# The second pair's keys turned on VectorE with unscaled tables, merged table products, zeros from ScalarE, one low weight part on VectorE, and a new order of all operations

## The chip, the cores and the metric

The kernel runs on one core of a Trainium2 chip. The metric is device microseconds of one execution; a median of three is given. TensorE is called PE in the rows, VectorE DVE, ScalarE ACT, GpSimd POOL, and the engine whose queue starts most transfers SP.

## What is computed

An attention over 8 batches and 8 heads (576 positions, 64 numbers a head) with rotary positions feeds a gated MLP. In short:

```python
q_rot, k_rot = (rotate(q), rotate(k))          # x1*cos - x2*sin, x1*sin + x2*cos
scores = scale * np.matmul(q_rot, k_rot.transpose(0, 1, 3, 2))
attn = softmax(scores)
x = np.matmul(attn, v)                          # heads side by side: (8, 576, 512)
h = np.maximum(x @ w_in, 0.0)                   # 512 -> 1024
u, v = (h[..., :512], h[..., 512:])
v_n = (v - mean(v)) / sqrt(var(v) + 1e-6)
v_s = einsum('ts,bsd->btd', w_spatial, v_n) + b_spatial
out = (u * v_s) @ w_out
```

## The kernel before

Heads are worked in 32 pairs, four pairs to a batch. A pair's q and k come transposed, 128 rows (two heads of 64) by 2 x 576 columns: the numbers and their swapped halves. The rotation is one product of all 1152 columns with the cosine and sine tables `tabs`, and one sum of the two halves of 576. Pairs 0 to 3 (`prepare_whole`, WHOLE = 4) feed plain float32 products; later pairs (`prepare`) are split into a high and a low part and stacked for three-term products. Scores of one tile (128 queries by 576 keys) fill two banks of PSUM, which has eight (`sc` buffers of two banks, `pm` buffers of one). On each tile VectorE takes the maximum (line 843) and ScalarE the exponential (line 846); only then are the banks free. For pairs 0 to 3 TensorE then transposes the weights (lines 684 and 687), VectorE or ScalarE copies them out (lines 693 and 695) and TensorE multiplies them with the values (line 730); later pairs use VectorE's transposes (line 848) and line 761. When the four pairs of a batch are done, `mlp` runs: lines 918 (v half), 941 (u half), 959 (spatial) and 974 (output), interleaved with the next batch's attention. The scaling by 1/8 is split between q and k: the tables are multiplied by the square root of 1/8 (line 643) once pair 0 has been turned, and pair 0's keys take the whole 0.125 instead.

The weights come as 64-bit numbers and are decoded by VectorE and ScalarE (`decode`), with a high part rounded by ScalarE and the rest subtracted on POOL (lines 468 and 469, through the helper at 423). `open_stacks` (line 397) fills two half tiles with zeros on POOL before pair 4. At the very start four matmuls on zeros (`wake`, line 1034) keep TensorE busy until the first scores.

Every operation is recorded in a list and then issued in the order of the text `ORDER`, one number per operation. A letter picks the engine where there is a choice (a ScalarE, v VectorE, g POOL); `HOME` gives the slot of each new buffer, PSUM banks included. Each engine, and each queue, takes its own operations in that order, so a waiting one holds back all that follow on its engine.

Of the kernel before, what the change touches and what calls it, by code (L numbers as in the profile page):

```python
# [40 lines left out]
DEC_O = [120.69, 119.26, 149.95, 144.74]  # L41
GATE_U = [2, 2, 3, 3]
# [58 lines left out]
0 2 4 6 5 1 3 7 12 66 10 8 9 139 11 143 16 14 17 140 309 13 15 71 72 77 75 73 74 76 82 80 81 145 78 79 18 87 60 61 141 85 86 83 84 88 89 90 219 144  # L101
146v 92 91 93 94 131 19 313 97 101 98v 215 102a 142g 37 20 21 148 151 149 113 114a 95 96a 311 99 100a 104 105a 150 132 22 110 111a 133 23 24 103 152
424 25 106 107a 108 109a 503 38 153 63 221 156 39 154 127 128a 122 157 155 28 40 41 42 43 123a 112 124 158 394 220 222 134 62 125a 216 147 29 217 159
117 118a 161 119 120a 135 30 31 115 160 162 32 33 34 121 126 129 315 223 163 314 116 166 64 130 171 164 175 172a 167 310 312 165 218 176v 317 35 168
169 170 173 174v 177 178a 224 227 207 180 316 182 181a 186 421 46 228 184 300 225 226 185v 187a 183a 208 179 209 47 48 136 189 190v 229 230 137 44 232
49 50 51 188 422 428 231 203 204a 233 138 191 192 195 196a 385 193 194v 429 234 200 432 436 198 199a 52 235 236 45 201v 434 435 197 202 26 237 239 205
242 238 206 240 247 248v 244 245 243 256 257v 210 241 249 253 55 27 246 211 212 213 283 437 251 433 258 254v 259a 250v 252a 291 292 293 284 318 260
262 255 261a 423 430 431 319 320 321 322 265 214 53 54 323 263a 264 266a 294 295 269 296 297 438 439 271 324 325 326 327 274 298 412 275a 267 285 426
272v 328 268 301 302 270v 276 277a 329 330 273 279 280a 278 748 754 755 331 341 332 749 756 757 286 342a 303 304 305 444 36 345 346a 442 306 307 308
333 334 335 336 337 338 339 340 377 443 281 343 344v 440 446 447 441 287 378 347 348a 413 448 379 450 494 451 359 360a 356 357a 282 288 458 459 354  # L110
355v 820 826 445 449 349 452 380 453 352 381 350 460 414 415 462 463 454 351a 353a 363 365 764 765 416 455 417 364a 464 358 373 466 366a 418 767 368
289 290 374a 467 461 768 456 369a 370 403 386 367 361 419 371a 372 375 468 362 457 420 387 376 465 382 821 470 758 469 759 478 471 427 472 383 479 384
# [210 lines left out]
def tile_attention_gated_mlp(  # L323
# [102 lines left out]
    win, wout = {}, {}  # L426

    def decode(key, where, at, src, after=()):

        n = f"w{'io'[where is wout]}" + "".join(map(str, at))  # L430
        tiles = {}
        sg = Buf("m", [P, HF], I32, f"sg{n}")
# [694 lines left out]
```

## Time and profile before

| what | value |
| --- | --- |
| median of 3 runs | 813.5 us (813.34 to 813.94) |
| the profiled execution | 812.71 us |
| its span, first to last instruction | 810.9 us |
| TensorE matmul busy | 797.8 us (98%) |
| TensorE weight loads | 720.8 us (89%) |
| POOL / VectorE / ScalarE busy | 610.0 / 579.5 / 538.9 us |
| granted TensorE clock | 1.00 of 2.4 GHz in every slice |

The span leaves 1.8 us of the execution outside. A matmul's end is modelled, so a busy TensorE can still hide short pauses; the time at which the next matmul begins is exact. A line can be that of a helper: 423 is every low part, 420 every rounding, 388 every fill.

### The profile page before, as it was taken

Reading aid. Unit: us, or ns where it says so; the run is one execution under the profiler, and the core shown is the slowest. Engines: PE = TensorE matmul, PEld = TensorE weight load, DVE = VectorE, ACT = ScalarE, POOL = GpSimd, SP = SyncE. Lnnn points to the kernel's source line nnn. Section 1 sums busy time; section 2 is a strip of 40 time slices with the busy share of each in tenths; the row PEclk is TensorE's granted clock in tenths of the full one; section 3 lists DMA queues with packets and bytes.
Section 4 is the critical chain, followed back from the end, with each engine's and each line's share of the span. In section 5 each row is a group of like instructions: output and inputs, shape, how many; then the busy total and the mean of one; then the engine's idle time right before and its main releaser. Section 6 shows DMA issues by size and latency. Waiting matters only on the chain.

```text
span 810.9 us, 30065 instructions
## 1 busy us (share of the span) xinstructions
PE 797.8 (98%) x12568; PEld 720.8 (89%) x12568; DVE 579.5 (71%) x1230; ACT 538.9 (66%) x1355; POOL 610.0 (75%) x507
## 2 busy tenths in 40 slices
PE   7999999999999999999999999999999999999998
PEld 3666699988999989999999988999799998999898
DVE  6989998858876587677866769876696758774310
ACT  5889797656865577556875668766576657754442
POOL 7979899877798777887878868888687869643222
PEclk9999999999999999999999999999999999999999
DMA  9855575566676575567656667566656766453101
GB/s 346 276 167 172 141 195 124 143 186 171 161 183 172 152 196 152 169 167 190 174 148 170 163 181 197 148 173 159 168 149 152 186 180 179 101 123 84 44 2 59
DMA packets 53818, 129.85 MB, mean 160 GB/s; under 512 B 7858, under 2 KB 9906, under 8 KB 53683
## 3 DMA queue, kind: packets, MB, share of 16 engines
q1 hardware_dynamic: 53138, 127.35, 57.0%
q8 instruction: 98, 1.61, 0.8%
q10 hardware_dynamic: 544, 0.59, 0.2%
q14 instruction: 38, 0.30, 0.1%
HBM read 93.55 MB, written 9.58 MB: 127 GB/s over the span
## 4 chain that ended last, share of the span: by engine, by line
PE 86%; DMA 6%; POOL 4%; ACT 2%; issue 1%; DVE 1%; SPq 1%; ACTq 0%; POOLq 0%; DVEq 0%
PE psum L801 16%; PE psum L761 15%; PE psum L959 15%; PE psum L941 13%; PE psum L974 12%; PE psum L918 10%; DMA st<-in_qk_dram 2%; POOL st L545 2%; PE psum L821 2%; PE psum L684 1%; PE psum L730 1%; DMA ws<-in_w_spT_dram 1%; POOL st L549 1%; DMA vr<-in_v_dram 1%; DMA stk<-lk 1%
## 5 line engine op out<-in xcount | busy, mean ns | idle before, releaser
L846 ACT ACTIVATE et<-psum,nmx 128x576 f32<-128x576 f32 x288 | 212.7, 740 | 103.0 <-DVE nmx L843 100.4
L843 DVE TENSOR_REDUCE nmx<-psum 128x1 f32<-128x576 f32 x288 | 212.2, 747 | 85.9 <-PE psum L801 68.4
L848 DVE STREAM_TRANSPOSE et<-et 128x576 f32<-128x576 f32 x252 | 186.4, 760 | 31.4 <-ACT et L846 30.3
L545 POOL TENSOR_TENSOR st<-st,tabs 128x1152 f32<-128x1152 f32 x56 | 149.6, 2671 | 23.4 <-DMA st<-in_qk_dram 21.7
L761 PE MATMUL psum<-et,vr 32*64 32x144 f32 x8064 | 142.0, 285 | 0.5 <-DMA vr<-in_v_dram 0.5
L761 PEld LDWEIGHTS psum<-et,vr 32*64 32x64 f32 x8064 | 126.6, 130 | 12.0 <-issue 8.9
L959 PE MATMUL psum<-wsp,vn 128*128 128x288 f32 x768 | 126.6, 296 | 1.1 <-issue 1.1
L941 PE MATMUL psum<-x,wi 128*128 128x288 f32 x768 | 124.5, 296 | 0.4 <-issue 0.4
L918 PE MATMUL psum<-wi,x 128*128 128x512 f32 x448 | 120.6, 395 | 0.0
L974 PE MATMUL psum<-g,wo 128*128 128x288 f32 x768 | 120.2, 296 | 0.4 <-POOL g L423 0.4
L941 PEld LDWEIGHTS psum<-x,wi 128*128 128x128 f32 x768 | 110.8, 188 | 5.7 <-issue 2.3
L959 PEld LDWEIGHTS psum<-wsp,vn 128*128 128x128 f32 x768 | 109.8, 188 | 2.9 <-issue 2.2
L974 PEld LDWEIGHTS psum<-g,wo 128*128 128x128 f32 x768 | 108.4, 188 | 3.9 <-issue 2.0
L801 PE MATMUL psum<-stk 128*128 128x288 f32 x448 | 99.0, 302 | 2.0 <-ACT et L846 1.5
L801 PE MATMUL psum<-stk,stk 128*128 128x288 f32 x448 | 95.8, 295 | 0.6 <-issue 0.6
L918 PEld LDWEIGHTS psum<-wi,x 128*128 128x128 f32 x448 | 78.3, 188 | 12.7 <-issue 1.4
L423 POOL TENSOR_TENSOR stk<-st,stk 64x512 fp32r<-64x512 f32 x56 | 71.9, 1284 | 21.5 <-ACT stk L420 10.7
L801 PEld LDWEIGHTS psum<-stk 128*128 128x128 f32 x448 | 72.5, 188 | 11.1 <-issue 3.3
L549 POOL TENSOR_TENSOR st<-st 128x576 f32<-128x576 f32 x56 | 79.8, 1427 | 3.4
L423 POOL TENSOR_TENSOR x<-x,x 128x576 fp32r<-128x576 f32 x64 | 54.5, 875 | 24.0 <-ACT x L420 22.0
L801 PEld LDWEIGHTS psum<-stk,stk 128*128 128x128 f32 x448 | 71.7, 188 | 0.8 <-issue 0.8
L423 POOL TENSOR_TENSOR g<-u,g 128x288 fp32r<-128x288 f32 x64 | 50.9, 808 | 25.9 <-ACT g L420 23.3
(130 smaller groups left out, 1063.7 us busy)
## 6 DMA issues: line engine op xcount, KB each, us to landing
vr<-in_v_dram SPq DMA_DIRECT2D x116, 320.0 KB
st<-in_qk_dram SPq DMA_DIRECT2D x62, 576.0 KB
stk<-lk SPq DMA_DIRECT2D x168, 144.0 KB
out_dram<-ob SPq DMA_DIRECT2D x31, 288.0 KB
ws<-in_w_spT_dram SPq DMA_DIRECT2D x2, 576.0 KB
tabs<-in_tab_dram ACTq DMA_DIRECT2D x2, 288.0 KB
st<-in_qk_dram SPq DMA_DIRECT2D x2, 288.0 KB
wi10raw<-in_w_in_dram SPq DMA_DIRECT2D x1, 512.0 KB
```

Of the source, the lines that this page charges most:

```text
L423: eng.tensor_tensor(out=lo, in0=src, in1=hi.bitcast(F32), op=ALU.subtract)
L545: f = lambda e: e.tensor_tensor(out=st[j][:, cols], in0=st[j][:, cols], in1=tabs[:, cols], op=ALU.mult)
L549: f = lambda e: e.tensor_tensor(out=st[j][:, :S], in0=st[j][:, :S], in1=st[j][:, S:2 * S], op=ALU.add)
L761: nc.tensor.matmul(bank(g)[64 * h:64 * h + 64, EACH // 9 * (1 - h):EACH // 9 * (1 - h) + EACH], lhsT=vr[rows, b % 4, b // 4, h, :], rhs=e[ ...
L801: nc.tensor.matmul(pt[:, c * 512:c * 512 + HALF], lhsT=lhsT, rhs=rhs[:, c * HALF:(c + 1) * HALF], start=(n == 0), stop=(n == len(parts) - 1))
L843: op(DVE, 680, key + K_MAX, lambda: nc.vector.tensor_reduce(out=nmx.tile, in_=tops(), op=ALU.max, axis=AX.XY, negate=True), r=[pt], w=[nmx ...
L846: op(ACT, 750, key + K_EXP, lambda: nc.scalar.activation(weights(), tops(turn), AF.Exp, bias=nmx.tile, scale=1.0, accum_out=sm[:, to:to + ...
L848: op(DVE, 705, key + K_TURN, lambda: nc.vector.transpose(out=blocks(et, at), in_=blocks(et, at)), w=[(et, at)])
L918: nc.tensor.matmul(pm.tile, lhsT=lhsT, rhs=win[1, d][:, j, :], start=(d == 0 and n == 0), stop=(d == 3 and n == len(todo) - 1))
L941: nc.tensor.matmul(pm[:, :HALF], lhsT=win[0, d][:, i, f * P:(f + 1) * P], rhs=x[d][:, at:at + HALF], start=(d == 0 and n == 0), stop=(d == ...
L959: nc.tensor.matmul(pm[:, :HALF], lhsT=lhsT, rhs=rhs, start=(t == 0 and n == 0), stop=(t == 4 and n == 1))
L974: nc.tensor.matmul(pm[:, :HALF], lhsT=wout[d,][:, i, m * P:(m + 1) * P], rhs=gs[d][:, at:at + HALF], start=(d == 0 and n == 0), stop=(d == ...
```

## The change

- The tables are scaled by one ScalarE instruction of 1152 columns, after pair 1 has been turned (before: two, of 384 and 768 columns, before pair 1). Pair 1's keys are turned by VectorE with the factor 0.125, both products in one instruction; its queries by POOL with the unscaled tables.
- For pairs 1 to 3 the two table products of a tile (576 columns each) become one of 1152. The sums stay; both of pair 1's sums are on POOL now.
- The zeros of `open_stacks` are written by ScalarE (a copy with factor 0) and not by POOL.
- The low part of one of the twelve weight tiles, (1, 3), is subtracted by VectorE, whose input stays in PSUM.
- ORDER and HOME are new throughout. At the start POOL clears the small tiles before the tile that `wake` reads; SP loads pair 1's q, its values, and then its k (before: k, q, and the values later); pair 0's values come after four weight tiles and three more tiles of q and k. VectorE takes pair 0's first maximum from head 0 (before: head 1), ScalarE's first exponential being head 0 in both. VectorE's order there is: maxima of tiles 0, 1 and 2 (two each), pair 1's key product, maxima of tile 3, the first step of a weight, the maximum of tile 4. The two-bank slot of tile 4 is the slot of the second half of pair 1's first scores. The table scaling stands on ScalarE behind tile 4's exponential and two copies from PSUM, and ahead of two more copies. TensorE has five groups of transposes of pair 0 ahead of pair 1's first scores (before: two groups).

```diff
-            fill(lks[0][64:P, :], 0.0)
-            fill(lks[1][0:64, :], 0.0)
+            for part in (lks[0][64:P, :], lks[1][0:64, :]):
+                nc.scalar.activation(part, tabs[0:64, :S], AF.Copy, scale=0.0)
...
-        op(POOL, 1800, 20 * WHOLE - 25, place, r=[("scored", i) for i in range(min(WHOLE, 2))], w=opened, new=wide)
+        op(ACT, 2 * act_ns(S), 20 * WHOLE - 25, place, r=["tabs", *[("scored", i) for i in range(min(WHOLE, 2))]], w=opened, new=wide)
...
+        here = where is win and at in PSUM_LOWS
...
-            round_hi(where[at][:, 0, :], value())
+            round_hi(where[at][:, 0, :], pt.tile if here else value())
...
+        if here:
+            op(DVE, 605, key, lambda: stt(out=pt.tile, in0=pt.tile, scalar=2.0**-20, in1=value(), op0=ALU.mult, op1=ALU.mult), r=[sg], w=[pt])
+            op(ACT, 495, key, high, r=[pt], w=[t0, t1, (n, "hi")])
+            op(DVE, 605, key, lambda: rest_lo(nc.vector, where[at][:, 1, :], pt.tile, where[at][:, 0, :]), r=[pt, (n, "hi")], w=[n])
+            return
...
-            for cols, toks in ((thirds[0], ["tabsA"]), (slice(Q0, S), ["tabsA", "tabs0", "tabs"])):
-                op(ACT, act_ns(2 * (cols.stop - cols.start)), -50, lambda cols=cols: nc.scalar.activation(c2(tabs)[:, :, cols], c2(tabs)[:, :, cols], AF.Copy, scale=0.125**0.5), w=toks)
         else:
+            table = ["tabsA", "tabs0", "tabs"]
             for j, st in ((1, k), (0, q)):
-                for c in range(2):
-                    cols = slice(S * c, S * c + S)
-                    pair_op(S, key - K_ROPE, lambda e, st=st, cols=cols: e.tensor_tensor(out=st[:, cols], in0=st[:, cols], in1=tabs[:, cols], op=ALU.mult), r=["tabs0", "tabs"], w=[(st, c)])
+                both = [(st, 0), (st, 1)]
+                if i == 1 and st is k:
+                    op(DVE, dve_ns(2 * S), 0, lambda st=st: nc.vector.scalar_tensor_tensor(out=st.tile, in0=st.tile, scalar=0.125, in1=tabs, op0=ALU.mult, op1=ALU.mult), r=table, w=both, port=True)
+                else:
+                    pair_op(2 * S, 0, lambda e, st=st: e.tensor_tensor(out=st.tile, in0=st.tile, in1=tabs, op=ALU.mult), r=table, w=both)
                 pair_op(S, key - K_SUM, lambda e, st=st: e.tensor_tensor(out=st[:, :S], in0=st[:, :S], in1=st[:, S:], op=ALU.add), w=[(st, 0), (st, 1)])
+            if i == 1:
+                op(ACT, act_ns(2 * S), -50, lambda: nc.scalar.activation(tabs, tabs, AF.Copy, scale=0.125**0.5), w=table)
```

## Rows read from the trace of the kernel before

**Rows 1.** Windows: stretch, length, busy us (instructions) of the five engines, clock, DMA share, GB/s
```profile
0.00:8.00 8.00, 6.46 (x12) 2.58 (x12) 2.62 (x6) 2.46 (x3) 3.72 (x16) 1.00 0.74 253
8.00:18.00 10.00, 7.08 (x40) 3.60 (x39) 8.28 (x15) 7.00 (x17) 9.10 (x8) 1.00 1.02 407
18.00:86.00 68.00, 68.00 (x543) 43.55 (x542) 62.22 (x111) 60.68 (x156) 61.50 (x46) 1.00 0.66 206
86.00:90.10 4.10, 2.34 (x16) 1.88 (x16) 3.95 (x7) 3.48 (x9) 3.54 (x5) 1.00 0.85 244
...
sum 811.00, PE 797.76 PEld 720.81 DVE 579.51 ACT 538.91 POOL 609.99; mean PE 99.72 PEld 90.10 DVE 72.44 ACT 67.36 POOL 76.25
```

**Rows 2.** Waits of TensorE after 18 us: total us, times, longest
```profile
PE psum L801 <- ACT et L846: 1.8, 2, 1.2
...
PE psum L974 <- POOL g L423: 0.4, 1, 0.4
```

**Rows 3.** Timeline of the start: start us, us, engine, line, operation, count, idle before
```profile
1.37 5.95 PE L1036 MATMUL psum<-wsp 128*128 128x512 f32 x8 [1.37 <-POOL wsp L388]
...
8.87 0.76 PE L821 MATMUL psum<-st,st 64*128 64x288 f32 x4 [0.63 <-DVE st L634]
...
9.77 1.41 DVE L843 TENSOR_REDUCE nmx<-psum 128x1 f32<-128x576 f32 x2
...
11.28 0.74 ACT L846 ACTIVATE et<-psum,nmx 128x576 f32<-128x576 f32 x1 [0.87 <-DVE nmx L843]
...
14.23 2.81 DVE L843 TENSOR_REDUCE nmx<-psum 128x1 f32<-128x576 f32 x4 [1.24 <-PE psum L821]
...
17.75 0.88 PE L684 MATMUL psum<-turns,et 128*128 128x128 f32 x6 [0.26 <-ACT et L846]
...
18.55 1.24 PE L821 MATMUL psum<-st,st 64*128 64x288 f32 x8
18.65 0.74 ACT L846 ACTIVATE et<-psum,nmx 128x576 f32<-128x576 f32 x1 [0.23 <-DVE nmx L843]
...
19.72 0.88 PE L687 MATMUL psum<-turns,et 128*64 128x128 f32 x12
...
26.62 1.51 PE L730 MATMUL psum<-turns,vr 128*64 128x384 f32 x8
```

**Rows 4.** Timeline of the start again: pair 1's products and sums on POOL and VectorE
```profile
10.49 5.48 POOL L649 TENSOR_TENSOR st<-st,tabs 128x576 f32<-128x576 f32 x4 [0.28 <-ACT tabs L643]
...
15.93 1.40 POOL L650 TENSOR_TENSOR st<-st 128x576 f32<-128x576 f32 x1
...
16.95 0.99 DVE L650 TENSOR_TENSOR st<-st 128x576 f32<-128x576 f32 x1
```

**Rows 5.** Groups by line and form: count, busy us, mean ns, idle before
```profile
L545 POOL TENSOR_TENSOR st<-st,tabs 128x1152 f32<-128x1152 f32 x56 | 149.6, 2671 | 23.4 <-DMA st<-in_qk_dram 21.7 <-PE psum L684 0.6
...
L693 ACT ACTIVATE turns<-psum 128x384 f32<-128x384 f32 x37 | 17.1, 492 | 3.4 <-PE psum L684 3.3
L649 POOL TENSOR_TENSOR st<-st,tabs 128x576 f32<-128x576 f32 x12 | 17.1, 1450 | 0.3 <-ACT tabs L643 0.3
...
L423 POOL TENSOR_TENSOR wi<-sgwi,wi 128x512 fp32r<-128x512 f32 x8 | 10.2, 1286 | 0.1
...
L467 DVE SCALAR_TENSOR_TENSOR sgwi<-psum,sgwi 128x512 f32<-128x512 f32 x8 | 5.5, 690 | 0.2
...
L388 POOL MEMSET stk<- 64x576 f32 x2 | 1.2, 578 | 0.1
...
L643 ACT ACTIVATE tabs<-tabs 128x768 f32<-128x768 f32 x1 | 0.8, 843 | 2.0 <-POOL st L621 2.0
L616 DVE SCALAR_TENSOR_TENSOR st<-st,tabs 128x576 f32<-128x576 f32 x1 | 0.8, 758 | 5.2 <-DMA st<-in_qk_dram 5.2
```

**Rows 6.** Timeline ahead of the first MLP: the last steps of pair 3 on POOL
```profile
86.29 1.40 POOL L884 TENSOR_TENSOR x<-x,rb 128x576 f32<-128x576 f32 x1 [1.62 <-ACT x L736]
...
88.55 1.70 POOL L423 TENSOR_TENSOR x<-x,x 128x576 fp32r<-128x576 f32 x2 [0.20 <-ACT x L420]
```

More of the change, by code (lines that the diff above doesn't have):

```diff
@@ L41 @@
 DEC_O = [120.69, 119.26, 149.95, 144.74]
+PSUM_LOWS = [(1, 3)]
 GATE_U = [2, 2, 3, 3]
@@ L100 @@
 ORDER = """
[L101 to L112, printed above, removed]
[126 rows of a table removed]
+5 2 0 64 4 6 7 8 9 14 140 144 141g 137 3 215 35 142g 17 307 304 10 11 44 12 13 15 16 69 70 1 71 72 73 74 75 80 26 78 76 83 79 81 77 85 405 84 99 95
@@ new lines @@
+138 82 100a 88 89 139g 86 87 18 19 90 91 92 129 96v 97 98a 111 112a 20 21 143 305g 216g 145 102 93 103a 22 94a 58 146 147 23 148 378 308g 149 212 106
+108 104 105a 101 213g 214 109v 396 130 131 59 107a 36 217 150 153 132 151 37 38 39 125 126a 154 120 121a 110 152 117 118a 40 41 27 122 123a 155 156
+158 115 113 116a 28 29 30 31 32 114 42 157 159 119 124 127 128 160 161 163 162 165 166 309 174 164 133 60 181 182v 175v 167 168 204 417 172 170 179
+173v 134 171a 205 206 420 415 219 222 418 183 169a 387 180a 177 218 220 176 414 223 421 422 186 221 24 178v 45 224 135 187v 53 200 136 61 25 184v 185
@@ new lines @@
+46 201a 225 190 226 192 306 427 428 47 227 228 193v 54 188 189 48 49 429 229 191a 195 196a 197 230 231 207 198v 33 194 50 51 295 199 234 232 425 430
+52 202 233 419 242 203 55 239 246 237 238 235 236 243v 247a 253 240 241 248 251 254v 249v 244 245a 34 255 252v 286 287 62 426 311 256a 208 257 312 314
+288 289 290 313 250 291 292 260 315 316 258a 259 319 317 487 278 209 210 261a 269 270v 279 280 416 423 424 742 211 293 320 318 266 267a 296 264 431
+432 262 321 322 271 263 265a 268 749 324 297 741 294 272a 310 298 299 274 323 275a 747 281 300 273 301 748 325 338 334 339a 335a 326 435 331 302 434
@@ L239 @@
+327 328 329 330 276 433 336 332 282 337v 439 440 333 340 813 277 341v 443 441 283 444 347 819 370 750 349 352 350a 371 445 451 348a 436 437 406 407
+343 344a 353a 372 373 447 452 342 453 408 442 345 438 346a 446 374 356 357a 409 448 284 455 358 410 359a 449 366 367a 757 759 456 457 351 411 363 459
+820 285 450 758 460 361 362a 364a 760 751 461 360 458 354 355 379 365 368 369 303 454 375 462 463 464 380 381 471 472 465 466 382 752 376 467 383 388
[126 rows of a table added]
 """
 HOME = (
-    "01070020712003011221130201201213760217011015263445506604050615010173614710047061155236501006170162062731000654701241567607400101120510504201"
@@ L242 @@
-    "65304710201601271652144723455011764610170102070601500101062530741215001420101226100026350104465014616714200101470124037000147550001031026011"
-    "15430500017054100102201003740110012061107000151430000100110641005221400000107106504110011144010016050040002503040001157600110040500107001036"
-    "00015004071160000020014710000100761125010101600040002030010150020710601401000111300015174010000070241301006170501413000213110406511400010250"
-    "10400011700061150101504710000156072300024001763001031054010011010371010140001000000701116000503010107001102060402170160100000751400311600051"
@@ L246 @@
-    "10401225746012001540007012000111006315110007461001010015740000220000165034115002117001610001015011070100000400101060000102701531114206001000"
-    "31151204070120047000012615040007100102013601470400021600011005004151700110016310600407010000100760151040121000116101720046110203001000700110"
-    "01254017010111000611530002165040000013005100041102701061501107111200400106221000170003115000160041457100060146000071000260110075114100011200"
-    "70601014000000600120010715204300610021100010102300011517400070004000000700113651040010617301032101041711010010060114504071500611100021507040"
@@ L250 @@
-    "00070200011065010704101012530610110000152100171030601051000001111700450036200045010110000160045000002011276010150040100216000530000004107064"
-    "5110500114136005707042657022476510315040211732564275604375014652674657306154261"
+    "01200711207312000103120120305400151017263001176454012476657007010116142606441001452072101027360150467230001006457315012467015164230643100011"
+    "52404602071610017154236475501160701264010010170012527400105016103404154020120172310007131154740564670105270341010724301710404607000112061154"
@@ new lines @@
+    "01232070005341010170120000161000504012170001361000114120104712610001000010710501613400072601200314701060000716003105040712106011040111005500"
+    "00021460067102200006105310010700006500011010160000211430005011000176100024110012300157001400000070001065010001110042165101114021063007100600"
+    "07410051035000107606041025000160002041003010051176200012415010103001100714002100003000071160100510734010123000160510410200015070061000001430"
+    "06510201007410340152700040001001001576100511400010060100654010001025307160100000115001140101030115010040000001721260001050010110046001713231"
@@ new lines @@
+    "10510174000110704010006151000071021600073041106172030010040110650141105760101120015700000000000741100611500011100072630040110710216000110015"
+    "00101006214070110001300015401070300204701000000116050074111002101140160005200004001001700604001155007420021506000074010001207615100001101001"
+    "14711005000101210740011061000511030041120010010201057034101107040010007101040016252007112120010371500400100007310014650100110546000161020054"
+    "00200000010150071610541101237051110007011002613500071041001100112410006112320005740010015040710000200101265001170004110051700110301034016147"
@@ L252 @@
+    "0501010504060060510547265023475610210235146207416507436217454667247506041562750"
 )
@@ L641, in prepare_whole @@
             op(DVE, 3 * dve_ns(Q0), -57, lambda: by_psum(q, thirds[2], 1.0, HALF), r=[pt], w=[(q, 2), "turning", part])
-            for cols, toks in ((thirds[0], ["tabsA"]), (slice(Q0, S), ["tabsA", "tabs0", "tabs"])):
-                op(ACT, act_ns(2 * (cols.stop - cols.start)), -50, lambda cols=cols: nc.scalar.activation(c2(tabs)[:, :, cols], c2(tabs)[:, :, cols], AF.Copy, scale=0.125**0.5), w=toks)
         else:
+            table = ["tabsA", "tabs0", "tabs"]
             for j, st in ((1, k), (0, q)):
-                op(DMA, dma_ns(576), key - K_LOADW - j, lambda j=j, st=st: load(st.tile, qk[b, hp, j].rearrange("p c n -> p (c n)")), w=[(st, 0), (st, 1)], new=[st])
-                for c in range(2):
-                    cols = slice(S * c, S * c + S)
-                    pair_op(S, key - K_ROPE, lambda e, st=st, cols=cols: e.tensor_tensor(out=st[:, cols], in0=st[:, cols], in1=tabs[:, cols], op=ALU.mult), r=["tabs0", "tabs"], w=[(st, c)])
+                both = [(st, 0), (st, 1)]
+                op(DMA, dma_ns(576), key - K_LOADW - j, lambda j=j, st=st: load(st.tile, qk[b, hp, j].rearrange("p c n -> p (c n)")), w=both, new=[st])
+                if i == 1 and st is k:
+                    op(DVE, dve_ns(2 * S), 0, lambda st=st: nc.vector.scalar_tensor_tensor(out=st.tile, in0=st.tile, scalar=0.125, in1=tabs, op0=ALU.mult, op1=ALU.mult), r=table, w=both, port=True)
+                else:
+                    pair_op(2 * S, 0, lambda e, st=st: e.tensor_tensor(out=st.tile, in0=st.tile, in1=tabs, op=ALU.mult), r=table, w=both)
                 pair_op(S, key - K_SUM, lambda e, st=st: e.tensor_tensor(out=st[:, :S], in0=st[:, :S], in1=st[:, S:], op=ALU.add), w=[(st, 0), (st, 1)])
+            if i == 1:
+                op(ACT, act_ns(2 * S), -50, lambda: nc.scalar.activation(tabs, tabs, AF.Copy, scale=0.125**0.5), w=table)
         load_values(vr, b, hp, key)
```

252 rows, old and new, of the table ORDER are left out of this document.

## Prediction

> **What bounds the kernel now.** I read the windows by stage first. TensorE's matmuls fill 797.76 of 811 us, so 13.2 us are all that any reordering can find [rows 1]. The reader is to see where these lie: 1.5 us in the first 8, 2.9 us from 8 to 18, nothing at all from 18 to 86, 1.8 us from 86 to 90.1, and by subtraction some 7 us in all the rest, the drain at the end among it. The granted clock is 1.00 in every stretch, the higher of its two levels. From 18 to 86 us the other engines are nearly full too: VectorE 62.22, POOL 61.50 and ScalarE 60.68 of 68 us [rows 1]. So that stretch has one bound and three engines close behind it.
>
> Then I read who makes TensorE wait after 18 us. The largest is 1.8 us in two waits of scores for an exponential [rows 2]; both lie between 86 and 90.1 us. There the first MLP waits for pair 3's output, which passes through POOL, ScalarE and POOL from 86.29 to 90.25 us, and TensorE has only four score tiles to fill that time with [rows 6]. POOL had been idle for 1.62 us before the first of these steps, so it is not late there: a lighter POOL doesn't shorten this chain. Of the later waits only 0.4 us has POOL as its releaser [rows 2].
>
> The start I read from the timeline, since the change has most of its edits there. The wake-up matmuls end at 7.32, the first scores follow, the first exponential starts at 11.28, and from 17.75 us on TensorE doesn't stop [rows 3].
>
> The profiled execution took 812.71 us for a span of 810.9; the median of the runs is 813.5. I make the sum as a difference and put it on the median, 0.8 us above the profiled one.
>
> **The change, part by part.** No edit takes work from TensorE, and none adds any. The number of matmuls is the same, and by the order's text TensorE enters the products of line 761, or leaves them, equally often (56 runs of half a pair each in both orders). So each edit counts only by the waits it makes or removes.
>
> POOL loses pair 1's key products, 2 x 1.45 = 2.9 us; 1.45 x 2 - 2.67 = 0.23 us in each of five merged products, 1.15 in sum; the zeros, 2 x 0.58 = 1.16; and one low part, 1.29. It gains one sum, 1.40, that VectorE did before [rows 4, 5]. That is 5.1 us less of POOL's work in the first 90 us. Its price on the path is nothing from 18 to 86 us, where TensorE has no pause to give back [rows 1].
>
> VectorE gains the key product of 1152 columns. Bounds are one and two times the row of 576 columns, 0.76 and 1.52 us; from 0.690 us for 512 columns to 0.758 for 576 it is some 1.06 ns a column, so I take 1.36 [rows 5]. It loses the sum of 0.99 us [rows 4] and gains a low part (0.69, as the nearest row of that size) and, by the letters in the order, two more copies from PSUM. That is about 2 us more in a stretch where it has 5.8 us idle [rows 1]. On the path I count that at nothing, except at the start (below); if the cover is gone, the upper end is the whole 2 us.
>
> ScalarE gains the zeros, two instructions that cost from 0.49 us (384 columns out of PSUM) to 0.84 us (768 columns) each [rows 5], and loses two copies at 0.49. The table scaling of 1152 columns lies between 0.84 and 1.69; from 384 to 768 columns it is 0.91 ns a column, so I take 1.2 [rows 5].
>
> Now the start. (a) The tile that the wake-up reads is cleared after the small tiles, so the wake-up moves later by about one fill of its kind, 0.58 to 0.7 us: 7.32 becomes 8.0. The first half of the first scores (0.76 us) then ends at 8.76, still ahead of the second half at 8.87, which waits for VectorE [rows 3]. Cost nothing, with 0.1 us of cover; without it, up to 0.7.
>
> (b) The maxima of the first tile end at 10.47 and 11.18, and the first exponential waited for the second of them. Head 0 goes first now, so the exponentials start at 10.53, 0.75 us sooner [rows 3].
>
> (c) Tile 2's maxima began 1.5 us after the second exponential ended (11.28 + 1.46 = 12.74 to 14.23) [rows 3]; now that is 11.99 + 1.5 = 13.5. Two maxima at 0.70 end at 14.9; the key product ends at 16.25; two maxima of tile 3 at 17.65; a weight's first step of 0.69 at 18.35; tile 4's maximum at 19.05; its exponential at 19.8. Before, that one ended at 18.65 + 0.74 = 19.4 [rows 3]. The key product, which stands ahead of tile 3's maxima, eats the 0.75 us and 0.4 more.
>
> (d) The second half of pair 1's first scores needs tile 4's banks, so it can't start before 19.8 and ends near 20.95. Before, these scores ran from 18.55 to 19.79 with two groups of transposes ahead (0.44 each), and the tails of 0.88 and one more group behind them, to about 21.0 [rows 3]. The new order has those five ahead. At 21 us both have done the same.
>
> (e) On ScalarE a small sum (0.2) and two copies follow tile 4's exponential, to 21.0, then the scaling, to 22.2, then the two copies that free the banks of TensorE's fourth and fifth group after pair 1's first scores: 22.7 and 23.2. TensorE, after three groups, would come to them at 22.2, so these groups end at 23.1 and 23.6 and not at 23.0: 0.6 to 0.8 us late. Nothing after it makes this good, as TensorE has no pause until 86 us; at the work that before began at 26.62 it would be some 0.8 us behind [rows 1, 3].
>
> (f) The loads move at 407 GB/s [rows 1]. Up to and with pair 1's k, 3.28 MB are ahead; 2.02 MB had moved by 8 us (253 x 8), so it is in by 8 + 1.26/0.407 = 11.1, and with a microsecond to land well before 14.9. Pair 0's values (6.9 MB) are in at some 21 us and needed at 23.6. Both queues' reorderings are hidden.
>
> So the start lies between -0.75 (only b counts, all later steps find cover) and +1.5 (0.8, and a's 0.7). No row is nearer to either end, so I take the middle, +0.4. The later wait on POOL of 0.4 us I let go, as POOL is 5 us ahead: -0.4. The wait from 86 to 90.1 us stays, because its chain is the same. Sum 0.0: 813.5 us.
>
> **A lock between VectorE and POOL.** VectorE's sum took 0.99 us while POOL's was still running (from 15.93 to 17.33); VectorE needs 0.758 us for as many columns with POOL waiting for a transfer [rows 4, 5]. So pair 1's key product may be held by POOL's product or sum of pair 1's q. POOL's products began at 10.49 after 0.28 us of waiting for the table scaling [rows 4]; now they can begin at 10.2 and end with the sum at 10.2 + 2.67 + 1.40 = 14.3, which is 0.6 us before the key product. The Trainium skill ("SBUF — State Buffer", section "Who interferes with whom") says that the two engines share one pair of ports and that whoever comes first holds it for the whole instruction. By that rule the key product, coming 0.6 us sooner than I have it, waits out POOL's sum; the trace agrees with a wait, 0.99 against 0.758, and the time that it would give is the second rival's below.
>
> **The rivals.** First, faster: POOL's 5 us do count. If pair 2's and pair 3's tiles come ready earlier, TensorE's order can have something to do in the 1.8 us before the first MLP, and the start gives its 0.75. That is 813.5 - 1.8 - 0.75 - 0.4 = 810.6 if all of it comes, and 811.6 if half of it and a little more does; I put the case at 811.4. For it speaks that POOL is the fullest helper after TensorE over the whole span (610 us) and that 7 us of small pauses lie after 90 us; against it the idle 1.62 us of POOL just before that chain [rows 6]. Chance 0.35.
>
> Second, slower: VectorE becomes late at the start and stays so. Place: the key product, if POOL's sum for pair 1's q ends after 14.9 us, which needs POOL to be 0.6 us later than in my sum. Price: the rest of a sum of 1.40 us added to the 0.8 of step (e), up to 2.2 us, and nothing gives it back before 86 us. It gives 815.7. For it speaks that VectorE has but 5.8 us of slack there and takes 2 more [rows 1]; against it the 0.6 us. Chance 0.24.
>
> Third, the change doesn't do what it says: only one of twelve low parts moves, and merging leaves the sums where they are, so POOL's relief could vanish into waits of its own. That is the forecast's time, 813.5, and is counted in it.
>
> **How the numbers follow.** A measurement of this kernel can tell about 0.2%, 1.6 us, from no change. The forecast, within that bound, has 0.41; its own range is 812.2 to 815.0 (813.5 with -0.75 - 0.4 and +1.5). Faster by over 0.2% 0.35, slower 0.24. With both rivals the range for eight in ten goes from 810.8 (the faster case with nearly all of it) to 815.7 (the slower one).
>
> **What would show it.** In the profile of the changed kernel: the first exponential near 10.5; the key product on VectorE near 14.9 with about 1.36 us (over 2 us would be the lock); tile 4's exponential near 19.1; pair 1's first scores ending near 21; a pause of TensorE near 22 to 23.6 behind the table scaling; TensorE without a pause from there to the last products of pair 3, and again 1.8 us of pauses before line 918 first runs. The prediction is wrong if TensorE's pauses in the windows sum to less than 11.5 us or more than 15 us, or if pauses come up in the middle, from 110 to 740 us, that before doesn't have: an order new throughout can make such pauses anywhere, and I have followed it by hand only through the start and the first MLP.

## The result, and the profile after

The changed kernel takes 817.2 us, the kernel before 812.0 us in the runs beside it: a ratio of 1.0056, with an interval from 1.0038 to 1.0075. So it is 5.2 us slower, where the forecast had no change and a range up to 815.7. The profiled execution took 816.87 us for a span of 815.0.

The windows of the changed kernel, in the columns of [rows 1]:

```profile
0.00:8.00 8.00, 5.79 (x12) 2.38 (x12) 2.76 (x6) 1.94 (x2) 3.29 (x14) 1.00 0.76 251
8.00:18.00 10.00, 7.89 (x44) 4.04 (x42) 9.01 (x16) 6.46 (x16) 7.39 (x7) 1.00 1.02 404
18.00:86.00 68.00, 67.47 (x533) 42.85 (x534) 62.83 (x113) 61.29 (x156) 59.73 (x40) 1.00 0.69 216
86.00:90.10 4.10, 2.32 (x15) 1.85 (x15) 3.45 (x7) 3.97 (x11) 3.49 (x5) 1.00 0.87 233
```

Up to 90 us hardly anything has changed: TensorE's sum over the four stretches is 83.5 us of matmuls, against 83.9 in [rows 1]. The waits of TensorE over the whole span (total us, times, longest) show what is new; these answer [rows 2]:

```profile
PE psum L771 <- issue: 1.8, 2, 1.0
PE psum L811 <- ACT et L856: 1.8, 2, 1.2
PE psum L969 <- ACT u L954: 1.4, 1, 1.4
PE psum L694 <- ACT et L856: 1.3, 1, 1.3
PE psum L984 <- POOL g L424: 0.8, 1, 0.8
```

The pause ahead of the first MLP (the second row) is the one of before. The fourth row is a pause at the start, for tile 3's exponential. The wait on POOL is 0.8 us where it was 0.4, instead of going. Two rows are new: 1.4 us for the first MLP's spatial product at 132 us, and 1.8 us in the value products (line 771) in which TensorE waits for nothing that the profile shows. The kernel before has 2.1 us of this last kind too, in other products; [rows 2] leave them out:

```profile
PE psum L959 <- issue: 1.1, 1, 1.1
PE psum L801 <- issue: 0.6, 1, 0.6
...
PE psum L941 <- issue: 0.4, 1, 0.4
```

**How far TensorE is behind, place by place.** Single pauses are easily over-read, so I worked out a lag from the trace: for each matmul the time from its start to the next one's, less the median of that for its line and shape in the kernel before, summed in the order of execution; the time ahead of the first matmul counts in the first stretch. Both kernels do the same 777 us of matmuls, so the lag can be compared where equal work is done. The table gives by how much it grows in each stretch, as a mean over the profiled executions (four of before, three of after; the other columns come from the experiments).

```
matmul work done   before  after   e8,e13   e12    e19    e2
   0 to  80 us      0.87    1.22    1.16    5.28   2.83   0.73
  80 to 125         5.10    5.12    5.44    4.61   5.15   6.17
 125 to 150         0.63    2.50    0.73    0.63   0.62   2.15
 150 to 235         5.49    4.08    3.97    4.17   5.15   3.88
 235 to 325         2.43    3.32    2.41    2.43   2.43   3.91
 325 to 360         1.36    2.74    2.67    1.34   1.36   1.69
 360 to 440         2.59    3.74    3.32    2.43   2.32   2.50
 440 to 480         2.18    1.03    0.97    3.13   1.93   1.03
 480 to 520         1.42    3.18    2.57    1.42   1.41   2.88
 520 to 777         8.13    8.36    7.86    7.73   8.44   8.94
 sum               30.2    35.3    31.1    33.2   31.6   33.9
```

The sums differ by 5.1 us, which is the loss that the times show. Executions of one kernel differ by up to 1.6 us in a stretch (in the first one, 0.1 to 1.3 us for before and 0.5 to 1.7 for after), so small differences tell nothing. The reader is to see that the start has 0.35 of the loss, that 1.9 come between 125 and 150, 1.4 at 325, 1.8 at 480 and about 1 each at 235 and 360, and that the kernel before has costs of its own that the new order avoids (1.4 at 150 to 235, 1.15 at 440 to 480).

### The profile page after: what moved, and what is told of

The parts are those of the page before. It is cut to its first block, busy times and chain, and to the rows that moved or that the text cites. A ratio compares the mean times of both kernels' runs of the same rounds, so it can differ in the third digit from the quotient of the medians.

```text
span 815.0 us, 30030 instructions
## 1 busy us (share of the span) xinstructions
PE 800.4 (98%) x12568; PEld 723.1 (89%) x12568; DVE 582.7 (71%) x1233; ACT 538.5 (66%) x1354; POOL 603.9 (74%) x498
## 4 chain that ended last, share of the span: by engine, by line
PE 88%; POOL 4%; DMA 3%; ACT 2%; issue 1%; DVE 1%; SPq 1%; POOLq 0%; DVEq 0%
PE psum L811 16%; PE psum L771 16%; PE psum L928 13%; PE psum L969 12%; PE psum L984 12%; PE psum L951 12%; PE psum L740 2%; PE psum L831 2%; DMA st<-in_qk_dram 2%; PE psum L694 2%; POOL st L552 1%; DMA vr<-in_v_dram 1%; ACT et L856 1%; DVE nmx L853 1%; PE psum L697 1%
## 5 line engine op out<-in xcount | busy, mean ns | idle before, releaser
L858 DVE STREAM_TRANSPOSE et<-et 128x576 f32<-128x576 f32 x252 | 188.4, 763 | 37.2 <-ACT et L856 35.7
L771 PE MATMUL psum<-et,vr 32*64 32x144 f32 x8064 | 143.8, 285 | 2.4 <-issue 1.8
```

What stands on the lines that cost most here:

```text
L771: nc.tensor.matmul(bank(g)[64 * h:64 * h + 64, EACH // 9 * (1 - h):EACH // 9 * (1 - h) + EACH], lhsT=vr[rows, b % 4, b // 4, h, :], rhs=e[ ...
L858: op(DVE, 705, key + K_TURN, lambda: nc.vector.transpose(out=blocks(et, at), in_=blocks(et, at)), w=[(et, at)])
```

## The experiments

Theory O: the new order of the work loses the time, by pauses of its own. Theory P: the changed instructions lose it.

### The parts alone and the order alone

e1: the changed instructions in the old order. The order's numbers are mapped one to one; each merged product stands where the second of its two pieces stood, and the scaling of the tables behind pair 1's products. (In this kernel the last weight block's rounded parts are read from a tile that other work has overwritten by then; e12 is without that.)

> The changed instructions in the order of the kernel before: pair 1's key product on VectorE with the unscaled tables, merged products, the tables scaled by ScalarE after pair 1's products, zeros by ScalarE, the low part of one weight block by VectorE. If the loss of 5 us comes from the new order (theory O), this stands within 1 us of the kernel before. If the changed instructions themselves cost it (theory P: the scaling ahead of evacuations, ScalarE's zeros, VectorE's extra work), it is 3 us or more slower than before.

Measured: 818.2 us, ratio 1.0078 [1.0055, 1.0101].

e2: the instructions of before in the new order.

> The instructions of the kernel before in the order and the buffers of the changed kernel (tables scaled first, each product in two pieces on GpSimd, zeros and the low part on GpSimd). Theory O: 3 to 5 us slower than the kernel before, with the TensorE waits of the changed kernel after 90 us (at 132 us for the first MLP's spatial product, at 168 us for a low part of the gate). Theory P: within 1 us of the kernel before.

Measured: 817.5 us, ratio 1.0064 [1.0049, 1.0079], with the waits of the changed kernel (0.6 us at 132, 0.8 at 168, 1.4 at 530 us).

So the order alone (with its buffers, which e2 moves along with it) loses as much as the whole change, as theory O has it. But the parts in the old order lose too, 6.3 us here and 3.5 in e12: neither theory had both. The table says where: the parts in the old order (e12) lose all of it in the first 80 us, the new order loses it behind them.

### Two first repairs

e3, in the text of the order (the numbers are operations: 891 is a table product, 572 the values' low part, 495 a weight's low part, 680 the gate's):

```diff
-... 891 ... 572 ... 495 ... 680 ...
+... 572 891 ... 680 495 ...
```

> The changed kernel with two places of GpSimd's order swapped: the low part of the normalised values ahead of the table product that waits for its load (at 129 us), and a low part of the gate ahead of a low part of a weight (at 167 us). If the two pauses of TensorE (1.4 and 0.8 us) stay in the end time, it is 1.5 to 2.2 us faster than the changed kernel, some 3 us behind before. If what comes later takes them up anyway, it stays within 0.5 us of the changed kernel, some 5 us behind before.

Measured: 817.2 us, ratio 1.0050 [1.0032, 1.0068]. The pause at 132 us is gone, but 0.6 us came up at 142.6 for another low part of POOL, 0.6 at 144.7, and 0.7 at 167.4, now for the weight's low part: POOL as a whole was late, and a swap only chose who waits.

e4 (138 is pair 1's key product, 86 and 88 tile 3's maxima, 143 the scaling, 103 and 94 the two evacuations, copies from PSUM):

```diff
-138 82 100a 88 89 139g 86 87 ... 143 305g 216g 145 102 93 103a 22 94a
+82 100a 88 89 86 138 139g 87 ... 145 102 93 103a 22 94a 143 305g 216g
```

> The changed kernel with its start reordered: pair 1's key product behind tile 3's maxima on VectorE, the scaling of the tables behind the two evacuations on ScalarE, the products of pairs 2 and 3 behind it. If the lag at 20 us (0.7 to 1.0 us) comes from these two and stays in the end time, it is about 0.8 us faster than the changed kernel. If GpSimd, which then gets its tables 0.9 us later, passes its own lag on, it is no faster.

Measured: 820.7 us, ratio 1.0093 [1.0073, 1.0114], 3 us worse. The key product had stood in a hole: without it, VectorE waits 0.96 us there for a buffer of maxima that an exponential still holds, so tile 3 gains nothing, while POOL's key sum comes 3.3 us later (19.32 against 16.05) and pair 1's scores wait for it.

### POOL's lateness at 125 us

e8 changes one place. In the changed kernel POOL's timeline (start, length, idle before and its releaser) is this:

```profile
124.54 1.42 POOL L556 TENSOR_TENSOR st<-st 128x576 f32<-128x576 f32 x1
129.17 2.66 POOL L552 TENSOR_TENSOR st<-st,tabs 128x1152 f32<-128x1152 f32 x1 [3.21 <-DMA st<-in_qk_dram]
131.78 1.27 POOL L424 TENSOR_TENSOR vn<-vv,vn 128x512 fp32r<-128x512 f32 x1
```

and SyncE's queue and TensorE's wait are these:

```profile
118.11 5.09 SPq L418 DMA_DIRECT2D st<-in_qk_dram  x2
...
133.54 0.67 PE L969 MATMUL psum<-wsp,vn 128*128 128x288 f32 x3 [1.42 <-ACT u L954]
```

The second of the two loads could be issued only at 122.84, when POOL's own low part of a stack (to 122.82) had given its buffer free; it landed at 129.1. POOL stood idle for it with the values' low part, ready since 128.3, queued behind the table product, and TensorE stood for that low part. (The row names ScalarE's `u`, which itself waited 2.26 us for POOL's `vn`.) The edit fills the hole (68 is a low part of the spatial weights, 894 a sum):

```diff
-... 894 ... 891 ... 572 ... 592 ... 68 ... 892 ...
+... 894 68 ... 572 891 ... 592 ... 892 ...
```

> The changed kernel with GpSimd's order changed in one place only: at 126 us, where it stands idle for 3.2 us until pair 7's query has landed, it first does the spatial weights' low part that it otherwise does at 134.5 us, then the low part of the normalised values, then the table product. GpSimd's work after it should come 1.4 to 2 us earlier. If its lateness between 125 and 170 us makes the loss, the pauses at 132, 146 and 168 us shrink and the kernel is 1.5 to 3 us faster than the changed kernel. If the loss comes from elsewhere, it stays.

Measured: 816.3 us, ratio 1.0047 [1.0032, 1.0063]; once more (e13) 815.9, ratio 1.0054 [1.0033, 1.0076]. POOL's timeline with the edit:

```profile
126.77 1.42 POOL L424 TENSOR_TENSOR wt<-wst,wt 1x576 fp32r<-1x576 f32 x1
129.17 1.28 POOL L424 TENSOR_TENSOR vn<-vv,vn 128x512 fp32r<-128x512 f32 x1 [0.98 <-ACT vn L421]
130.41 2.65 POOL L552 TENSOR_TENSOR st<-st,tabs 128x1152 f32<-128x1152 f32 x1
```

The stretch from 125 to 150 falls from 2.50 to 0.73 us in the lag, to within 0.1 of before. The pause at 167 us stays, with 1.0 us. By the ratios the times fall by about 1 us against the changed kernel, less than the 1.5 to 3 us expected, and the intervals overlap; the profiled executions of e8 and e13 were shorter than their medians, so their sum of 31.1 flatters them.

> The kernel with the one place of GpSimd's order changed (e8), unchanged, for a second profile: its profiled execution was among its shortest (813.6 us against a median of 816.3). If GpSimd's earlier work also removes the later waits of the changed kernel (an output at 281 us, a low part at 328 us, the gate's low part and a value load at 455 to 458 us, a value load at 628 us), they are missing again and only the pauses with nothing awaited (341, 528, 579 us) have grown. If they were missing by chance, they are back.

In e13 the waits at 281, 328 and 628 us are missing again, those at 452 to 455 us are back. So POOL's earlier work doesn't cure the last. That it cures the first three isn't shown: the changed kernel's first profile lacks those at 281 and 328 us too, and e16 that at 628.

e10 adds two more moves (1271 and 1272 are a table product and its sum, 680 is the gate's low part; 2242 is a load, 1928 another transfer):

```diff
-... 1271 1272 ... 680 ...      -... 2242 1928 ...
+... 680 1271 1272 ...          +... 1928 2242 ...
```

> The kernel of the run with one place of GpSimd's order changed (e8), and two more places: pair 9's table product and sum behind the gate's low part for which TensorE waited 1.0 us at 167 us, and the load of pair 16's key behind the transfer of the reciprocal sums, so that the piece of instructions fetched at 340 us finds the transfer engines free. Expected where pauses add up to the loss: the pauses at 167 us (1.0 us) and 341 us (1.1 us) gone, the kernel 1.5 to 2.5 us faster than with the one place, some 2 us behind the kernel before. Expected where a pause that is removed only comes back later: no faster than with the one place.

Measured: 818.3 us, ratio 1.0090 [1.0061, 1.0118]. The first move backfired: the table product and its sum (4.1 us) now stand ahead of another of the gate's low parts.

```profile
PE psum L984 <- POOL g L424: 3.0, 1, 3.0
```

The second did next to nothing: the pause came again at 345 us, with 0.9 us, so that load wasn't what held it.

### The pauses without a releaser

e5 and e16 are the changed kernel, e6, e14 and e15 the kernel before, all unchanged, for more profiles.

> The changed kernel once more, unchanged. If its pauses belong to the order of the work, TensorE stops again at the same places (some 1.4 us at 132 us for the spatial product, 0.8 us at 168 us for the gate, about 1 us each at 342 and 531 us in the value products of a pair, with nothing awaited) and the loss against the kernel before is again 4 to 6 us. If they are chance of one execution, they are elsewhere.

Measured: 817.6 us, ratio 1.0063 [1.0039, 1.0086].

> The kernel before once more, unchanged, for a second profile of it. The profiled execution shown first was one of the longer ones (813.3 us against a median of 812.0 with the later runs). If its pauses with nothing awaited (1.3 us at 243, 0.8 at 582, 0.6 at 413 us) belong to its order they come again; if they depend on when the loads pass, some are gone and the span is 1 to 3 us shorter.

> The kernel before for a third profile, since both profiled executions of it (813.3 and 815.3 us) were longer than its median (about 812). If the new order loses by pauses of its own between 120 and 560 us, a shorter execution of before differs from its longer ones in the start and in the pauses with nothing awaited (243, 413, 582 us), and has none of the pauses of the changed kernel at 132, 342, 455 and 531 us. If its executions differ everywhere a little, no place can be named.

> The same once more, for a fourth profile, with the same expectations.

> The changed kernel for a third profile. If its loss has places, TensorE's lag against the kernel before grows again at 131 us (by 1 to 1.5 us), at 342 us (1 to 1.6), at 455 to 458 us (0.8) and at 531 us (1.2 to 1.6), and shrinks at 243 and 413 us, where only the kernel before pauses.

Measured, in us, with each pause's excess over a matmul's usual interval:

```
before (812.7, 815.3, 812.9, 813.2):  243: 1.3 0.8 1.1 1.4   413: 0.6 0.3  -   -    582: 0.8 1.7 0.6 1.0
after  (816.9, 818.8, 818.9):         342: 1.1 1.6 1.1       531: 1.2 1.6 2.3       582: 0.3 0.8 0.5
```

(The expectations give the first time as 813.3; the execution whose profile is shown took 812.7.) The places recur, the lengths vary. The means of the sums are 2.4 us for before and 3.6 for after. Of the places expected of e16, that at 131 us came with only 0.5 us.

All these pauses have one thing in common. The records of TensorE's stream, counted from its start, leave the same remainder at each of them: 192 by 256 (within two). And the stream is loaded in pieces; this is the page's row of the queue that loads instructions (packets, MB, share):

```profile
q8 instruction: 99, 1.62, 0.9%
```

99 pieces of 16384 B; TensorE's 25 300 records are just under 99 times 256. The pause at 531 us in the changed kernel, and the same place of the stream in the kernel before, where there is none (TensorE's timelines):

```profile
529.11 2.22 PE L771 MATMUL psum<-et,vr 32*64 32x144 f32 x122
532.27 0.71 PE L771 MATMUL psum<-et,vr 32*64 32x144 f32 x22 [0.95 <-issue]
```

```profile
526.61 2.51 PE L761 MATMUL psum<-et,vr 32*64 32x144 f32 x144
```

In both, the piece that ends there lasted, but for the pause, only 2.8 to 2.9 us, since these short matmuls go by at 17 ns each. In the changed kernel the transfer of the next piece began 1.42 us after TensorE had entered this one and TensorE went on 2.6 us after that; in the kernel before it began 1.75 us ahead of it. The Trainium skill ("Runtime: NRT & Kernel Launch", section "Instruction fetch mechanics") says that each engine's instructions come in blocks of 16 KiB, 256 instructions, over a DMA queue of its own, and calls the cost of a boundary mostly hidden. The traces agree on the blocks; the cost is not always hidden. At each of the 19 pauses of the table TensorE went on 2.35 to 3.04 us after the next block's transfer had begun, so it stopped where that transfer began too late for the end of the block. Where there was time, it didn't stop: at 504 us in the kernel before, the transfer began 1.40 us after TensorE had entered a block that lasted 3.95 us. e9 shifts the whole stream, e17 does the same to the kernel before:

```diff
+        for _ in range(56):
+            nc.tensor.matmul(idle.tile[:, :32], lhsT=wsp[:, 0, 0, :P], rhs=wsp[:, 0, 0, :32], start=True, stop=True)
```

> The changed kernel with 56 matmuls of 32 columns more in the stretch in which TensorE warms up and waits for its first loads, so that every later instruction stands 112 places further on in TensorE's stream; nothing else changes. The pauses with nothing awaited all lie at positions that leave the same remainder (192) by 256, and the instructions are loaded in pieces of 16384 B. If a piece that is loaded too late makes these pauses, other stretches of short matmuls are now cut by the ends of pieces: reckoned from the trace, 10 to 35 us more pauses, at new places. If they have another cause, the time stays within 1 us of the changed kernel.

> The kernel before with 56 matmuls of 32 columns more in the warm-up, as in the run of the changed kernel with the shifted stream (848.2 us). If the places of the ends of instruction pieces are a property of any order and both orders happen to lie well, it loses as much: 20 to 35 us, and its pauses at 243, 413 and 582 us are gone while many others come. If only the changed order is open to it, it stays within 5 us of the kernel before.

Measured: 848.2 us and 839.8 us, one execution each. Their waits of TensorE (e9, then e17):

```profile
PE psum L771 <- issue: 6.6, 7, 3.1
PE psum L928 <- issue: 2.4, 1, 2.4
PE psum L811 <- issue: 2.3, 3, 1.2
PE psum L951 <- issue: 2.2, 2, 1.5
PE psum L984 <- issue: 2.1, 2, 1.1
```

```profile
PE psum L761 <- issue: 10.2, 10, 1.7
```

Of e9's pauses 21 us lie at the ends of its pieces, of e17's 19, where the unshifted kernels have 3.6 and 2.4. So the ends of the pieces make these pauses, in either order, and both orders lie well. But the shift isn't all of the loss of 31 and 27 us. The 56 matmuls were not hidden: they stand ahead of the first scores and hold them up. Their rows and the windows in which they run (e9, then e17):

```profile
7.74 9.86 PE L1048 MATMUL psum<-wsp 128*128 128x32 f32 x56
8.00:18.00 10.00, 10.00 (x59) 9.82 (x59) 0.31 (x1) 0.00 (x0) 6.02 (x6) 0.64 1.02 399
```

```profile
6.71 7.30 PE L1038 MATMUL psum<-wsp 128*128 128x32 f32 x56
8.00:18.00 10.00, 9.80 (x63) 8.27 (x64) 3.37 (x8) 0.90 (x2) 8.89 (x8) 0.73 1.02 405
```

The first scores start at 17.5 and 13.95 us and not at 7.4 and 7.5, and at the first MLP TensorE is 10.9 and 8.3 us late. That leaves some 20 and 19 us behind it, of which about 17 are added pauses at the ends of pieces. e9's mean granted clock is 0.988: half of what is missing lies in the 10.2 us at the lower level from 10.9 us on, which began while the idle matmuls ran, the other half at the pauses of 501 and 697 us. What holds up a piece's transfer isn't settled: loads were under way at 340 us (the transfer engines were 98% busy from 340.0 to 342.4), but e10, with one load fewer there, had the pause all the same.

### What the parts are worth

e11, the changed kernel with zeros and the weight block's low part back on GpSimd:

```diff
-PSUM_LOWS = [(1, 3)]
+PSUM_LOWS = []
-                nc.scalar.activation(part, tabs[0:64, :S], AF.Copy, scale=0.0)
+            fill(lks[0][64:P, :], 0.0)
```

> The changed kernel with two of its parts undone in the same order: the zeros of the stacks are set by GpSimd again, and the low part of the weight block is done by GpSimd again. If GpSimd's relief is worth anything, this is 0.5 to 2 us slower than the changed kernel, with more waits on GpSimd at 86 to 170 us. If the two parts are a burden to ScalarE and VectorE, it is 0.5 us or more faster. If they lie beside TensorE's work, it is within 0.5 us.

Measured: 818.8 us, ratio 1.0087 [1.0058, 1.0116]: if anything, these two parts help, by 1.1 to 1.6 us in the medians and 1.9 to 2.5 by the ratios; the intervals overlap with the changed kernel's.

> The changed instructions in the order of the kernel before, as in the first run of that kind, but with the low part of the weight block on GpSimd, so that no tile is overwritten early. If the start's parts (key product on VectorE, merged products, scaling after them) cost the time where the order was not made for them, it is again 5 to 6 us slower than before, and TensorE is 4 us or more behind when 80 us of matmuls are done. If the overwritten tile made the waits, it is within 2 us of the kernel before.

Measured: 815.2 us, ratio 1.0043 [1.0025, 1.0061], 3.5 us slower and not 5 to 6. TensorE is, as expected, 4.4 us further behind than in before at 80 us of work, and gains 1.4 of it back later. One row of e12 tells of the lock that the prediction weighed:

```profile
L655 DVE SCALAR_TENSOR_TENSOR st<-st,tabs x1: 2223/2223/2223, 12.9 to 12.9; 128x1152 f32<-128x1152 f32 x1
```

There pair 1's key product starts at 12.92, while POOL's product runs (11.31 to 13.93), and takes 2.22 us. In the changed kernel it starts at 14.62, clear of POOL, and takes 1.35. Waiting until 13.93 and then 1.35 would end at 15.28; it ended at 15.14.

e18 and e19 move three instructions of e12's start (138 the key product, 81 and 88 maxima, 82 and 89 exponentials, 143 the scaling):

```diff
-138 83 84 81 82 86 87 88 215 141 142v 90 89 91 ... 94a 143 97
+83 84 81 138 141 82 143 86 87 88 215 142v 90 89 91 ... 94a 97          (e18)
+83 84 81 82 86 87 88 138 141 215 142v 90 89 143 91 ... 94a 97          (e19)
```

> As the run of the changed instructions in the order of the kernel before (e12, low part on GpSimd), with three instructions moved in its start: pair 1's key product from ahead of tile 2's maxima to behind them (clear of GpSimd's own product, beside which it took 2.2 us), and the scaling of the tables from 21.9 us to behind the exponentials of tile 2 (about 16 us), so that GpSimd, which waited 6.5 us for the tables, goes on at about 17 us. If the start alone made e12's loss, TensorE is at most 1 us behind the kernel before when 80 us of matmuls are done, and the kernel is 2.5 to 5 us faster than e12: between 1.5 us slower and 1.5 us faster than the kernel before. If the instructions cost time wherever they stand, it stays 3 us or more behind before.

> The same with the key product behind tile 3's maxima and the scaling behind its exponentials, so that no maximum of pair 0 waits for the key product and GpSimd gets its tables at about 18.5 us, as late as it started these products in the kernel before (18.0 us). Expected as for e18; of the two, this is the faster by up to 0.7 us if the key product's 1.35 us ahead of tile 3's maxima delay TensorE, and the slower if pair 1's first scores, whose key sum comes 1.4 us later, do.

Measured: 815.0 and 814.0 us, ratios 1.0031 [1.0017, 1.0045] and 1.0026 [1.0012, 1.0039]. So the three moves were worth 1.0 and 1.4 us by the ratios, 0.2 and 1.2 in the medians, where 2.5 to 5 were expected (the intervals overlap with e12's). The start is only half mended, TensorE being 2.0 us behind before at 80 us in both: in e18 the key product and the scaling, now ahead of tile 3, stop TensorE for 2.0 us at 17.6, in e19 the late key sum for 1.9 us at 18.5. No version is faster than the kernel before.

## Why the prediction was wrong

**Step (a), right.** The wake-up began later, at 1.8 us, and was hidden; it also took 5.22 us and not 5.95, so the first scores start at 7.43 and not at 8.0.

**Steps (b) to (d), right in their times.** Lines of the changed kernel's start, to set beside [rows 3, 4]:

```profile
10.40 0.74 ACT L856 ACTIVATE et<-psum,nmx 128x576 f32<-128x576 f32 x1 [3.51 <-DVE nmx L853]
14.62 1.35 DVE L655 SCALAR_TENSOR_TENSOR st<-st,tabs 128x1152 f32<-128x1152 f32 x1
18.28 0.55 PE L694 MATMUL psum<-turns,et 128*128 128x128 f32 x3 [1.26 <-ACT et L856]
18.69 0.75 ACT L856 ACTIVATE et<-psum,nmx 128x576 f32<-128x576 f32 x1
19.56 1.25 PE L831 MATMUL psum<-st,st 64*128 64x288 f32 x8
20.41 1.16 ACT L660 ACTIVATE tabs<-tabs 128x1152 f32<-128x1152 f32 x1
20.74 2.19 PE L694 MATMUL psum<-turns,et 128*128 128x128 f32 x15
21.46 0.87 ACT L703 ACTIVATE turns<-psum 128x384 f32<-128x384 f32 x2
21.65 2.64 POOL L657 TENSOR_TENSOR st<-st,tabs 128x1152 f32<-128x1152 f32 x1 [4.20 <-ACT tabs L660]
```

Foretold were 10.53, 14.9 with 1.36, 19.1 (19.8 for its end, measured 19.4), 21 for the end of pair 1's scores (20.8), and 1.2 for the scaling. There was no lock, for POOL's sum ended at 14.0. POOL's 4.2 us of waiting for the tables, which the last row shows, I had not written down: TensorE paused only 0.25 us in all from 18.3 to 86 us, so little or nothing of it reached the path.

**Step (e), wrong, and its sum right by luck.** The scaling began at 20.4 and not at 21, the two copies behind it ended at 22.3 and not at 23.2, and TensorE went through its five groups (the fifteen matmuls) without the 0.6 to 0.8 us of pause, to 22.9. Its one pause was earlier, 1.26 us for tile 3's exponential, and I hadn't written it down. At the work that before began at 26.62 us I had TensorE some 0.8 us behind; it came to it at 26.55, ahead if anything:

```profile
26.55 1.51 PE L740 MATMUL psum<-turns,vr 128*64 128x384 f32 x8
```

The start's lag of +0.4 then measured +0.35 at 80 us, but the changed kernel lost this between 35 and 60 us (0.6, 0.7 and 1.7 us in its three profiles, nothing in the four of before), and the executions scatter by more than the difference. In one of the three, ScalarE's copies came late at 48 to 50 us (pauses of 0.8 and 0.5 us); in the other two no single pause of note stands there.

**Step (f), right.** No wait of TensorE in the start has a load as its releaser.

**The term of -0.4, wrong: the later wait on POOL.** I let the 0.4 us wait on POOL for the gate go, "as POOL is 5 us ahead" at 90 us. The longest such wait was 0.8, 0.9 and 0.9 us in the three profiles, and in the kernel before it varies from none to 0.9. POOL's lead at 90 us had no use 40 us later: between 107 and 130 us POOL stood idle for 5.6 us, 3.2 of them for a load whose buffer POOL itself gave free late. The lead of this engine, which works in a fixed order, wasn't kept: it was spent at its next waits.

**The step that failed: everything after 90 us counted as -0.4.** I took the order there as it was in before, and said that I had followed it by hand only to the first MLP. Its own pauses made 4.8 of the 5.1 us: +1.9 by POOL's lateness at 131 to 147 us (e8 removes it in the trace), +1.2 by late instruction pieces at new places, and the rest, 1.7, which is only a remainder: there are small waits for POOL and ScalarE at 281, 328 and 445 to 458 us, and before has its own at 465 and 487 us. The pauses without a releaser (2.1 of the 7 us that the prediction left for "all the rest") were there to be read in before's trace; the prediction counted none of them and put no price on their moving. The sign by which the prediction said it would be wrong came true: pauses between 110 and 740 us that before lacks, and sums of TensorE's pauses of 14.6, 16.4 and 17.3 us (its bound was 15; the execution shown first is within it). Two slips change nothing: the lower end of its own range comes to 812.35 and not 812.2, and POOL had another 0.2 us of TensorE's waits after 18 us, for scores.

**The rivals.** The faster one, POOL's relief, is in the trace (603.9 us of work against 610.0) but the time doesn't show its worth: e11 takes back half of it (zeros and low part, 2.45 of 5.1 us) and the loss, up to 2.5 us, isn't clear of the intervals. The slower one named the right sign with the wrong place: the lock at the start did not come, and the loss is one that no rival had. "The change doesn't do what it says" I had counted as no change; the relief did vanish into POOL's own waits, but the order took more.

What stays open: what holds up the instruction pieces at 342 and 531 us, and how much of the order's loss each place is worth in the time. Only the place at 131 us was removed by an edit. Nor are the order and the buffers that moved with it told apart.

## What to carry to other kernels

A new order of a kernel that is bound by one engine has to be costed over its whole length, queue by queue: a part's price is set by where it stands, and the same instructions cost 0.35 us in one start, which is inside the scatter, and 4.4 in another. Look for the instruction that waits for a load at the head of a queue, and ask what is queued behind it. Where an engine runs through hundreds of short instructions, count where its stream's blocks of instructions end before adding or removing any.

## What the hardware showed

- TensorE's instructions come in pieces of 256, and at the end of a piece used up in 2.8 to 6.2 us it stops for 0.3 to 2.3 us if the next one's transfer starts late; it goes on 2.35 to 3.04 us after that start. 112 places of shift added about 17 us of such pauses to either kernel.
- In one of the three profiles of the changed kernel the granted clock fell to its lower level, 1.2 GHz, for 3.4 us after the two pauses that ended at 88.3 and 89.7 us, and in two it didn't, though the pauses were the same (1.3 and 0.8 us); in that stretch the lag is 1.5 us longer. The windows, of the profile shown first and of e5:

```profile
90.10:93.70 3.60, 3.60 (x12) 3.04 (x12) 3.60 (x6) 2.24 (x5) 3.60 (x5) 0.53 0.43 104
```

```profile
90.10:93.70 3.60, 3.04 (x16) 2.64 (x17) 3.57 (x7) 2.84 (x6) 3.60 (x4) 1.00 0.29 72
```
